# Windowed attention with a gated FFN on one core: own list scheduler for every engine, attention by half sequences

## The chip, the cores and the metric

The kernel runs on one core of one Trainium2 chip. The metric is the device time of one execution in microseconds (us), the median of several. A profiled execution has a span, from its first to its last instruction, about 2 us shorter than the time of that same execution. Engines: PE (TensorE), ACT (ScalarE), DVE (VectorE), POOL (GpSimd), SP (issues most DMAs); SPq is SP's DMA-issuing queue.

Each run is marked fast or slow, slow when it is more than 1.5% above the fastest run of the same kernel in its rounds; a single run's state is unknown. The rounds ran on different chips (1, 2 and 15), so versions of different rounds are compared by their ratios to the kernel before, which ran in every one of them.

## The reference, cut to what matters

Eight sequences of 576 tokens, 8 heads of 64. Attention sees 32 tokens to each side. Its output, as 512 columns, goes through a gated FFN: `h = relu(x w_in)` with 1024 columns, a depthwise convolution over three tokens, a sigmoid of that as a gate, and `w_out`.

```python
scores = q @ k.T / sqrt(64);  mask: |i - j| <= 32;  x = softmax(scores) @ v     # per head
h = maximum(x @ w_in, 0)
conv[t] = sum_k conv_w[k] * h[t + k - 1]
out = (h * sigmoid(conv)) @ w_out
```

Inputs and output are float32. The kernels compute in bfloat16. q, k and v are 9.4 MB each.

## The kernel before

Each batch's q and k are loaded four heads at a time, v in five blocks of 128 rows. POOL casts them to bfloat16. PE transposes q and k against an identity, computes scores for 64-query tiles against 128 keys ("sc", two at a time in the two halves of the array's rows), ACT takes the exponential, DVE multiplies by the mask, PE multiplies by V ("av", 64 output rows each), DVE divides by the sum. The FFN runs in 12 chunks of 384 tokens: ph (w_in), pc (convolution as matmuls with diagonal weights), py (w_out). A job list with start times, in part kept in program order, sets the order; the framework's scheduler does the rest.

The q/k load, whose rows matter most here. The source's outermost count is 128 and so is the tile's:

```python
def load_qk(b, y, i):
    src = (q, k)[y][b, 4 * i:4 * i + 4, :, :]
    fixed(nc.sync.dma_start(
        qkst[y][i].rearrange("p e j d -> p e (j d)"),              # 128 partitions
        bass.AP(src.tensor, src.offset, [[RP * D, 128], [2 * S * D, 2], [1, RP * D]]),
    ))                                                             # RP = 9: rows of 2304 bytes
```

PSUM is one buffer of three banks for scores and transposes, and five single banks.

The softmax here doesn't subtract the row's maximum and nothing guards it: scores larger than these inputs give would overflow.

Of the kernel before, what the change touches and what calls it, by code (L numbers as in the profile page):

```python
# [10 lines left out]
FP32 = mybir.dt.float32  # L11
BF16 = mybir.dt.bfloat16
AF = mybir.ActivationFunctionType
ALU = mybir.AluOpType


@with_exitstack
def kernel(
# [24 lines left out]
    RP = S // 64  # L43
# [3 lines left out]
    apool = ctx.enter_context(tc.tile_pool(name="apool", bufs=3))  # L47
    fpool = ctx.enter_context(tc.tile_pool(name="fpool", bufs=2))
    spool = ctx.enter_context(tc.tile_pool(name="spool", bufs=3))
    psum_a = ctx.enter_context(tc.tile_pool(name="psum_a", bufs=1, space=bass.MemoryType.PSUM))  # L50
    psum_f = ctx.enter_context(tc.tile_pool(name="psum_f", bufs=5, space=bass.MemoryType.PSUM))

    NLD = 2
    NPH = NP // 2
    qkst = [[pp.tile([128, 2, RP, 64], FP32, name=f"{n}st{i}") for i in range(NPH)] for n in "qk"]
    vst = pp.tile([128, NBLK, H, 64], FP32, name="vst")
    qkb_pp = [
        [[pp.tile([128, RP, 2, 64], BF16, name=f"{n}b{i}{j}") for j in range(NPH)] for n in "qk"]
        for i in range(NLD)
    ]  # L60
    ve_pp = [pp.tile([128, NBLK, H, 65], BF16, name=f"ve{i}") for i in range(NLD)]
    vo_pp = [pp.tile([128, NBLK - 1, H, 65], BF16, name=f"vo{i}") for i in range(NLD)]
    NKT = 4
    kT_pp = [pp.tile([128, S + 2 * PAD], BF16, name=f"kT{i}") for i in range(NKT)]
    hT_pp = [pp.tile([128, MB, CH + (4 if i == 1 else 2)], BF16, name=f"hT{i}") for i in range(3)]

    w_in_sb = consts.tile([128, KC, d_ff], BF16, name="w_in_sb")
    w_out_sb = consts.tile([128, MB, d_model], BF16, name="w_out_sb")
    conv_w_sb = consts.tile([128, 3, MB], FP32, name="conv_w_sb")
    diag_w = consts.tile([128, 3, MB, 128], BF16, name="diag_w")  # L70
    ident = consts.tile([128, 128], BF16, name="ident")
    mask = consts.tile([128, 2 * S], BF16, name="mask")
    mask1 = consts.tile([128, NT, 64], BF16, name="mask1")

    fixed = tc.keep_in_program_order

    class InOrder:


        on = False  # L80

        def __init__(self, engine):
            self.engine = engine

        def __getattr__(self, name):
            do = getattr(self.engine, name)
            return (lambda *args, **kwargs: fixed(do(*args, **kwargs))) if InOrder.on else do  # L87

    vector, scalar, tensor = InOrder(nc.vector), InOrder(nc.scalar), InOrder(nc.tensor)

    def load_v(b, c):

        lo = 128 * c - PAD
        s0, s1 = max(0, lo), min(S, lo + 128)
        fixed(nc.sync.dma_start(  # L95
            vst[s0 - lo:s1 - lo, c, :, :], v[b, :, s0:s1, :].rearrange("h p d -> p h d")
        ))

    def load_qk(b, y, i):


        src = (q, k)[y][b, 4 * i:4 * i + 4, :, :]
        fixed(nc.sync.dma_start(
            qkst[y][i].rearrange("p e j d -> p e (j d)"),
            bass.AP(src.tensor, src.offset, [[RP * D, 128], [2 * S * D, 2], [1, RP * D]]),
        ))

    def cast(out_, in_):
        fixed(nc.gpsimd.tensor_scalar(  # L109
            out=out_, in0=in_, scalar1=1.0, scalar2=0.0, op0=ALU.mult, op1=ALU.add  # L110
        ))

    def load_stream(b):

        i = b % NLD
        ve, vo = ve_pp[i], vo_pp[i]

        def cast_v(c):
            cast(ve[:, c, :, 0:64], vst[:, c, :, :])
            if b == 0 and c > 0:  # L120
                vector.tensor_copy(vo[0:64, c - 1, :, :], ve[64:128, c - 1, :, :])
                vector.tensor_copy(vo[64:128, c - 1, :, :], ve[0:64, c, :, :])

        of_qk = [
            (lambda y=y, j=j: load_qk(b, y, j),
             lambda y=y, j=j: cast(qkb_pp[i][y][j].rearrange("p j e d -> p e j d"), qkst[y][j]))
            for j in range(NPH) for y in range(2)
        ]
        of_v = [(lambda c=c: load_v(b, c), lambda c=c: cast_v(c)) for c in range(NBLK)]
        return of_qk + of_v  # L130

    def shift_v(b):

        ve, vo = ve_pp[b % NLD], vo_pp[b % NLD]
        for p0, src in ((0, ve[64:128, 0:NBLK - 1]), (64, ve[0:64, 1:NBLK])):
            fixed(nc.sync.dma_start(vo[p0:p0 + 64], src))
# [4 lines left out]
    loads0 = list(load_stream(0))  # L141
    for ld, _ in loads0:
        ld()
    conv_w24 = consts.tile([3 * MB, 128], FP32, name="conv_w24")
    nc.scalar.dma_start(conv_w24, moe_conv_w.rearrange("k (m p) -> (k m) p", p=128))
    make_identity(nc, ident)
    ident24 = consts.tile([3 * MB, 3 * MB], FP32, name="ident24")
    nc.vector.tensor_copy(out=ident24, in_=ident[0:3 * MB, 0:3 * MB])
    nc.vector.memset(mask1, 1.0)
    nc.gpsimd.affine_select(  # L150
        out=mask1, in_=mask1, compare_op=ALU.is_ge, fill=0.0, base=0,
# [3 lines left out]
        out=mask1, in_=mask1, compare_op=ALU.is_ge, fill=0.0, base=64,  # L155
        pattern=[[0, NT], [1, 64]], channel_multiplier=-1,
    )
    nc.vector.memset(mask1[0:PAD, 0, :], 0.0)
    nc.vector.memset(mask1[128 - PAD:128, NT - 1, :], 0.0)
    for e in range(2):  # L160
        nc.vector.tensor_copy(
            out=mask[:, 512 * e:512 * e + 512], in_=mask1[:, 0:8, :].rearrange("p t x -> p (t x)")
        )
        nc.vector.tensor_copy(out=mask[:, 1024 + 64 * e:1088 + 64 * e], in_=mask1[:, 8, :])
    for t_ in ve_pp + vo_pp[0:1]:
        nc.vector.memset(t_[:, :, :, 64], 1.0)
    for t_ in kT_pp:
        nc.vector.memset(t_[:, 0:PAD], 0.0)
        nc.vector.memset(t_[:, PAD + S:], 0.0)
    nc.vector.memset(hT_pp[0][:, :, 0], 0.0)  # L170
    nc.vector.memset(hT_pp[1][:, :, HW + 1:HW + 3], 0.0)
    nc.vector.memset(hT_pp[2][:, :, CH + 1], 0.0)
    def make_diag(m):
        for kk in range(3):
            vector.tensor_scalar(
                out=diag_w[:, kk, m, :], in0=ident,
                scalar1=conv_w_sb[:, kk, m:m + 1], scalar2=None, op0=ALU.mult,
            )

    def load_weight(src, dst, rows, cast_):  # L180

        n = src.shape[1] // 2
        for x in (0, n):
            st = {}

            def load(x=x, st=st):
                t_ = fpool.tile([128, rows * n], FP32, name="wst", tag="wst")
                st[0] = t_.rearrange("p (c f) -> p c f", c=rows)
                fixed(nc.sync.dma_start(
                    st[0], src.rearrange("(c p) f -> p c f", p=128)[:, :, x:x + n]  # L190
                ))

            def casts(x=x, st=st):
                step = 512 // n
                for c in range(0, rows, step):
                    cast_(dst[:, c:c + step, x:x + n], st[0][:, c:c + step])

            yield load, casts


    def slot_a():
        return psum_a.tile([128, 1536], FP32, name="pa", tag="pa")

    def slot_f():
        return psum_f.tile([128, 512], FP32, name="pf", tag="pf")

    xT, xn = {}, {}
    state = {}

    def job_tr(g2, y):  # L210

        b, i = g2 // NPH, g2 % NPH
        nat = qkb_pp[b % NLD][y][i]
        to = []
        for g in (2 * g2, 2 * g2 + 1):
            if y == 0:
                t_ = apool.tile([128, S], BF16, name="qT", tag="qT", bufs=4)
                to.append(t_)
            else:
                t_ = kT_pp[g % NKT]  # L220
                to.append(t_[:, PAD:PAD + S])
            state["qk"[y], g] = t_

        small = b == 0
        for js in ((range(0, 4), range(4, 8), range(8, RP)) if small else (range(RP),)):
            j0, n = js[0], len(js)
            ps = slot_f() if small else slot_a()
            for j in js:
                tensor.matmul(  # L229
                    ps[:, 128 * (j - j0):128 * (j - j0) + 128],  # L230
                    nat[:, j, :, :].rearrange("p e d -> p (e d)"),
                    ident, start=True, stop=True,
                )
            rows = ps[:, 0:128 * n].rearrange("p (j y x) -> p y x j", j=n, y=2)
            for x, copy in enumerate((scalar.copy, vector.tensor_copy)):
                copy(  # L236
                    out=to[x].rearrange("p (x j) -> p x j", j=RP)[:, :, j0:j0 + n], in_=rows[:, x]
                )

    def job_conv_w():  # L240
        ps = slot_f()
        tensor.matmul(ps[:, 0:3 * MB], conv_w24, ident24, start=True, stop=True)
        vector.tensor_copy(out=conv_w_sb.rearrange("p k m -> p (k m)"), in_=ps[:, 0:3 * MB])

    def head(pr, e):
        return 4 * (pr // 2) + pr % 2 + 2 * e
# [336 lines left out]
```

## Time and profile before

| | before |
|---|---|
| time, median of 3 runs | 275.63 us (274.66 to 276.86) |
| span of the profiled run | 271.7 us |
| PE busy | 236.4 us, 87% |
| DMA traffic | 49.6 MB |

From the page of the kernel before: PE's busy time, then busy tenths in 40 slices of 6.8 us (9 is 90% or more); PEclk is the clock granted to PE in tenths, DMA the busy share of 16 engines.

```profile
PE 236.4 (87%) x2535; PEld 143.5 (53%) x2562; DVE 160.5 (59%) x362; ACT 175.3 (65%) x370; POOL 81.0 (30%) x96
...
PE   1736974786999978998999999999999999999994
...
PEclk9999998998999997999999999999999999999998
DMA  7999999997377986399959988967546114312123
```

PE is at 9 from about a quarter of the span on. In front of that it is busy a little over half of the time, and there DMA is at 7 to 9: the start waits for bytes. The chain of waits of the first 50 us (start us, length us, what) says the same:

```profile
...
8.21 6.40 DMA vst<-in_v_dram
14.70 14.20 DMA kst<-in_k_dram
29.28 4.91 DMA vst<-in_v_dram
34.92 9.19 DMA vo<-ve
...
```

And this is the DMA view of 2 to 12 us, 40 slices of 0.25 us each. The q/k loads are in flight in its first half, then v:

```profile
DMA  8669999999999999999999999999999999999999
GB/s 94 203 251 412 378 341 406 406 424 406 406 387 378 406 378 406 387 378 406 415 396 415 415 387 362 328 287 221 188 211 193 164 154 206 218 216 220 216 218 216
```

During q/k loads the share reaches 9 tenths of 16 engines, at about 400 GB/s. The 256-byte rows of v come at about 215.

For the whole span the chain is PE's:

```profile
...
PE 68%; DMA 15%; DVE 5%; SPq 4%; ACT 3%; issue 2%; POOL 0%
...
```

### The profile page before, as it was taken

How to read it: one execution, taken by the hardware profiler on the slowest of the kernel's cores; microseconds unless marked ns; L12 is line 12 of the kernel's file. 1: busy time of each engine (PE TensorE's matmuls, PEld its weight loads, DVE VectorE, ACT ScalarE, POOL GpSimd, SP SyncE). 2: the span in 40 equal slices, each digit the busy share in tenths (PEclk: the TensorE clock that was granted, in tenths of full speed). 3: DMA queues.
4: the chain of work that ended last, by engine and by line, in shares of the span. 5: the costliest groups of instructions: out<-in, count | busy, mean ns of one | idle time of the engine just before them, and what ended most of it. 6: DMA issues, size and time to landing. Idle time of an engine off the chain costs nothing.

```text
span 271.7 us, 6447 instructions
## 1 busy us (share of the span) xinstructions
PE 236.4 (87%) x2535; PEld 143.5 (53%) x2562; DVE 160.5 (59%) x362; ACT 175.3 (65%) x370; POOL 81.0 (30%) x96
## 2 busy tenths in 40 slices
PE   1736974786999978998999999999999999999994
PEld 1625543574665544554555556565656455555551
DVE  5797385895466673765766656676666562323230
ACT  2755572585577663876777777777778567657552
POOL 5758656873026201233323432322300000000000
PEclk9999998998999997999999999999999999999998
DMA  7999999997377986399959988967546114312123
GB/s 258 256 344 358 198 296 321 224 309 164 100 183 253 222 151 165 110 287 242 208 146 319 159 196 257 294 112 177 152 121 89 40 41 109 98 39 77 41 77 116
DMA packets 70498, 49.64 MB, mean 183 GB/s; under 512 B 53676, under 2 KB 55748, under 8 KB 70468
## 3 DMA queue, kind: packets, MB, share of 16 engines
q1 hardware_dynamic: 70432, 49.22, 70.6%
q8 instruction: 20, 0.33, 0.6%
q14 instruction: 10, 0.08, 0.1%
q10 hardware_dynamic: 36, 0.01, 0.0%
HBM read 32.52 MB, written 9.44 MB: 154 GB/s over the span
## 4 chain that ended last, share of the span: by engine, by line
PE 68%; DMA 15%; DVE 5%; SPq 4%; ACT 3%; issue 2%; POOL 0%
PE pf L405 22%; PE pf L349 20%; PE pf L387 14%; DMA kst<-in_k_dram 5%; PE pa L229 4%; DMA vst<-in_v_dram 4%; PE pf L282 4%; DMA vo<-ve 3%; PE pa L257 3%; DMA xT<-xn 3%; SPq L95 2%; DVE attn L268 1%; SPq L312 1%; DVE gT L392 1%; DVE diag_w L87 1%
## 5 line engine op out<-in xcount | busy, mean ns | idle before, releaser
L392 DVE SCALAR_TENSOR_TENSOR gT<-tn,hT 128x384 bf16<-128x384 f32 (+1 forms) x96 | 55.7, 585 | 55.7 <-ACT tn L391 55.6
L349 PE MATMUL pf<-xT,w_in_sb 128*128 128x385 bf16 (+2 forms) x380 | 73.6, 317 | 4.9 <-DMA xT<-xn 3.7
L405 PE MATMUL pf<-w_out_sb,gT 128*128 128x512 bf16 x261 | 66.5, 385 | 1.7 <-issue 0.4
L387 PE MATMUL pf<-hT,diag_w 128*128 128x384 bf16 (+1 forms) x288 | 59.0, 314 | 0.7 <-ACT hT L360 0.6
L349 PEld LDWEIGHTS <-w_in_sb 128*128 128x128 bf16 x380 | 34.4, 98 | 25.9 <-issue 3.3
L410 ACT COPY y_sb<-pf 128x512 f32<-128x512 f32 x36 | 21.1, 586 | 40.8 <-PE pf L405 40.8
L391 ACT ACTIVATE tn<-pf 128x384 f32<-128x384 f32 (+1 forms) x96 | 44.9, 469 | 2.3 <-PE pf L387 1.9
L109 POOL TENSOR_SCALAR ve<-vst 128x512 bf16<-128x512 f32 x40 | 28.9, 724 | 55.2 <-DMA vst<-in_v_dram 42.9
L405 PEld LDWEIGHTS <-gT 128*128 128x128 bf16 x288 | 28.0, 99 | 30.4 <-issue 1.6
L387 PEld LDWEIGHTS <-diag_w 128*128 128x128 bf16 x288 | 26.1, 98 | 17.1 <-issue 1.2
L369 ACT ACTIVATE hT<-pf 128x385 bf16<-128x385 f32 x56 | 27.7, 496 | 10.8 <-PE pf L349 10.1
L266 ACT ACTIVATE attn<-pa 128x1088 bf16<-128x1088 f32 x26 | 27.9, 1074 | 4.7 <-PE pf L257 3.9
L109 POOL TENSOR_SCALAR qb<-qst 128x1152 bf16<-128x1152 f32 x16 | 19.9, 1242 | 26.8 <-DMA qst<-in_q_dram 26.8
L268 DVE TENSOR_TENSOR attn<-attn,mask 128x1152 bf16<-128x1152 bf16 x26 | 20.9, 804 | 10.4 <-ACT attn L267 9.6
L109 POOL TENSOR_SCALAR kb<-kst 128x1152 bf16<-128x1152 f32 x16 | 18.9, 1182 | 21.9 <-DMA kst<-in_k_dram 21.1
L301 DVE TENSOR_TENSOR xn<-pf,rec 128x320 bf16<-128x320 f32 x52 | 24.3, 486 | 0.8
L364 ACT ACTIVATE hT<-pf 128x386 bf16<-128x386 f32 x24 | 11.9, 494 | 4.4 <-PE pf L349 4.0
L282 PEld LDWEIGHTS <-attn 128*64 128x64 bf16 x520 | 10.7, 112 | 7.3 <-issue 5.6
L282 PE MATMUL pf<-ve,attn 128*64 128x65 bf16 x312 | 13.8, 199 | 0.3 <-DVE attn L268 0.3
L257 PEld LDWEIGHTS <-kT 64*128 64x128 bf16 x468 | 9.0, 95 | 7.9 <-issue 5.5
L257 PE MATMUL pa<-qT,kT 64*128 64x64 bf16 x442 | 12.3, 191 | 0.9 <-DVE kT L236 0.9
L282 PE MATMUL pf<-vo,attn 128*64 128x65 bf16 x208 | 12.9, 200 | 0.0
(84 smaller groups left out, 240.1 us busy)
## 6 DMA issues: line engine op xcount, KB each, us to landing
qst<-in_q_dram SPq DMA_DIRECT2D x16, 576.0 KB, 6.4
kst<-in_k_dram SPq DMA_DIRECT2D x16, 576.0 KB, 7.4
out_dram<-y_sb SPq DMA_DIRECT2D x36, 256.0 KB, 2.2
vst<-in_v_dram SPq DMA_DIRECT2D x24, 256.0 KB, 4.7
vo<-ve SPq DMA_DIRECT2D x14, 260.0 KB, 7.8
vst<-in_v_dram SPq DMA_DIRECT2D x16, 192.0 KB, 5.0
wst<-in_moe_w_in_dram SPq DMA_DIRECT2D x2, 1024.0 KB, 8.4
wst<-in_moe_w_out_dram SPq DMA_DIRECT2D x2, 1024.0 KB, 8.9
```

What stands on the lines that cost most here:

```text
L109: fixed(nc.gpsimd.tensor_scalar(out=out_, in0=in_, scalar1=1.0, scalar2=0.0, op0=ALU.mult, op1=ALU.add))
L257: tensor.matmul(last[:, 0:64] if e * t == NT - 1 else ps[:, col(e, t):col(e, t) + 64], kT[64 * e:64 * e + 64, 64 * t:64 * t + 128], qT[64 ...
L266: scalar.activation(attn[:, 0:x], ps[:, 0:x], AF.Exp, bias=0.0, scale=scale)
L268: vector.tensor_tensor(out=attn, in0=attn, in1=mask, op=ALU.mult)
L282: tensor.matmul(pss[e][64 * j:64 * j + 64, 65 * c:65 * c + 65], attn[:, col(e, t):col(e, t) + 64], (ve if t % 2 == 0 else vo)[:, t // 2, h ...
L301: vector.tensor_tensor(out=to, in0=po[:, :, 0:64], in1=rec[:, :, None].broadcast_to([128, NBLK, 64]), op=ALU.mult,)
L349: tensor.matmul(ps[:, 0:n], w_in_sb[:, kc, m * 128:(m + 1) * 128], x_[:, kc, x0:x1], start=(kc == 0), stop=(kc == KC - 1),)
L369: scalar.activation(hT[:, m, o0:o0 + n], ps[:, 0:n], AF.Relu, bias=0.0, scale=0.5)
L387: tensor.matmul(ps[:, 0:n], diag_w[:, kk, m, :], taps(kk), start=(kk == 0), stop=(kk == 2))
L391: scalar.activation(tn[:, 0:n], ps[:, 0:n], AF.Tanh, bias=0.0, scale=1.0)
L392: vector.scalar_tensor_tensor(out=gT[c][:, m, HW * halves[0]:HW * halves[0] + n].rearrange("p (i x) -> p i x", x=HW), in0=tn[:, 0:n].rearr ...
L405: tensor.matmul(ps, gT[c][:, m, 128 * i:128 * i + 128], w_out_sb[:, m, :], start=(m == 0), stop=(m == MB - 1),)
```

## The change

Its intent: PE should start earlier and never wait. All instructions become operations of a plan; a list scheduler in the kernel places each at the earliest time by costs fitted to traces, chooses among allowed engines and PSUM banks (any of 8), and emits them in exactly that order. Attention goes by half sequences of 288 tokens, so that the FFN can begin after half a sequence; head g stands beside head g + 4. A few jobs change engine: the diagonal weights go to POOL, the V shift of sequence 1 goes from DMA to DVE. The diff, cut to its core:

```diff
-    qkst = [[pp.tile([128, 2, RP, 64], FP32, ...) for i in range(NPH)] for n in "qk"]
+    st = [[pp.tile([128, 2, RP, D], FP32, name=f"{n}st{s}") for s in range(2)] for n in "qk"]
+    ps_all = psum.tile([128, 8 * 512], FP32, name="ps_all")
...
+    def load_qk(b, y, s, prio):                # half s of all heads; NP = 4, HS = 288, RP = 9
+        src = (q, k)[y][b]
+        for h_ in range(2):
+            add(sp(), prio + 0.01 * h_, lambda e, h_=h_: nc.sync.dma_start(
+                st[y][s][:, h_].rearrange("p j d -> p (j d)"),
+                bass.AP(
+                    src.tensor, src.offset + HS * D * s + NP * S * D * h_,
+                    [[S * D, NP], [RP * D, 32], [1, RP * D]],
+                ),
+            ), writes=[("st", y, s, h_)], dma=0.77)
...
+    def transposes(b, s):                      # copies out of PSUM
+        copy(e, o_, ps(sl, 128 * a, 128 * (a + n)).rearrange("p (j g x) -> p g x j", j=n, x=32))
...
+    def values(b, s, g, t):                    # one PE group for each half and head pair
+        add(("PE", 0.02 * 4 * n), t, mm, ..., alloc=sl, slots=[sl], group=gr)
...
+    with tc.manual_schedule():
+        for op in plan.place():
+            op.run(op.eng)
```

## The prediction

> **What bounds the kernel now.** Span 271.7 us; runs take about 4 us more (median 275.6). The windows show two stages. From 64 to 264 us PE is 97% busy. In the first 64 us it is busy 39 us, with modelled ends, so I recount by start-to-start distances in the timeline: 216 ns for a 512-column matmul, 163 for 384, 56 for 128, about 18 for an attention matmul (they overlap in pairs). [...] In the first 30 us the trace shows 107 ns for 128 columns[...]. All matmuls at these distances come to about 211 us (estimate), so about 61 us are lost: 38 by 64 us, 10 to 16 from there to 260, 8 at the end.
>
> Why 38: the chain of waits is nearly all DMA up to 44 us (V load 6.4, K load 14.2, V load 4.9, the vo shift of sequence 1 9.2 us). DMA is nearly saturated there (about 0.27 MB per us), so what counts is the order of bytes. The first FFN matmul starts only at about 24 us because all of sequence 0 comes first; PE stands still from 40 to 44; until 68 it waits on evictions, one 3-bank buffer shared by transposes and scores, and 9 us of diag_w on DVE.
>
> **What the change does.** Matmul work, bytes and evicted elements stay nearly equal. It moves:
> - Half sequences: estimate from 0.27 MB/us: half 0 in at 9 us, w_in at 16, half 1 at 22, w_out at 29, sequence 1 at 35 and 42. First FFN matmul at about 16 us.
> - The b=1 vo shift goes from DMA (9.2 us) to DVE copies (0.3 us each); diag_w to POOL.
> - PSUM: any of 8 banks, no single 3-bank buffer. ACT loses 32 exponentials of 64 columns (0.22 us each), off the critical path.
> - Order on every engine fixed by a model whose costs match the trace (DVE 384 elements 476 ns, ACT 512 elements 489).
>
> **Sum.** With loads in at about 42 us, PE cannot have done more than chunks 0 and 1 and two sequences (38 us of work) by about 52; I expect 18 to 20 us lost by then, against 34 now: about 15 saved. Steady state (17.6 us of PE work per chunk; ACT about 67%, DVE 60%) should lose 6 to 10 after 52 instead of about 18: 8 to 10 saved. Tail (three output tiles, 5.2 us of matmuls, copy, store) unchanged. Total about 24: span 247, time 251 us, range 242 to 263.
>
> Chances: faster by over 2% 0.91, within 2% 0.06, slower 0.03.
>
> **What would show it.** First w_in matmul at 14 to 18 us; no PE hole near 40; PE slices at 9 from about 48 us; last chunk's start about 20 us earlier; chain without vo DMA before 50 us and almost all PE after; PE busy still about 236. POOL gains about 7 us (diag_w), DVE loses about 9.
>
> **What would make it wrong.** A fixed order that the chip's DMA does not follow: loads later than the plan's 0.77 us per 295 KB[...]. [...] diag_w on POOL could take longer than its 2.4 us and delay the casts. SP issues in order, so a store or transpose that waits can hold up loads. Those push to 263 or above.

Of the prediction are cut: a formula for the distance between matmuls, a cause given for the 107 ns (the clock granted in those 30 us is 1.00 of full speed), and two risks that rested on the same cause or on a mechanism that is not shown. That a store that waits can hold up loads is in the trace of before: from 58.8 to 69.9 us SPq issues nothing; then comes the store of what ACT has just copied, and 0.06 us after that issue a V load.

## The result, and the profile after

The kernel after takes 380.94 us (median of 4 runs, 380.15 to 381.59) against 275.14 us in the same rounds. The ratio is 1.383, 95% interval 1.377 to 1.389. Here and below a ratio is the mean of one kernel's fast runs over that of the other's fast runs in the same rounds, so not quite the ratio of the medians. The result is correct. It is 38% slower where 9% faster was forecast.

```profile
PE 264.3 (70%) x2618; PEld 156.8 (41%) x2618; DVE 168.5 (44%) x394; ACT 174.9 (46%) x348; POOL 71.9 (19%) x86
...
PE   0246526748492790592199937978769899999996
...
PEclk9999865867967796597589975989969999999999
DMA  2564375444455434736984369595369621321112
```

Now PE has holes over three quarters of the span, and DMA is mostly at 3 to 6, not at 9. Both are waiting. The DMA's half share is no sign of slack, as the view of 2 to 12 us shows beside that of before:

```profile
DMA  0221132122222222222235998322222222222368
GB/s 0 37 37 46 37 74 65 65 101 101 92 92 101 101 92 92 101 92 111 92 122 177 256 259 190 93 92 92 111 92 111 92 101 101 101 101 92 119 182 225
```

Wherever only q/k packets run, the share is 2 tenths and the rate 92 to 101 GB/s. Counted packet by packet in the trace, 4.2 are in flight at a time in these stretches, against about 16 in the kernel before. A packet is the same in both (2304 bytes, a median of 95 ns, before 93). So in these stretches a quarter as many packets move at a time. The chain of waits of the whole execution:

```profile
...
DMA 34%; SPq 32%; PE 23%; issue 3%; POOL 3%; DVE 2%; ACT 2%; POOLq 0%; ACTq 0%
SPq L369 14%; DMA qst<-in_q_dram 10%; SPq L344 9%; PE ps_all L739 8%; DMA kst<-in_k_dram 7%; DMA vst<-in_v_dram 7%; DMA out_dram<-y 7%; PE ps_all L668 7%; PE ps_all L698 6%; SPq L397 4%; DMA xT<-xn 2%; SPq L571 2%; SPq L412 2%; POOL qn L252 1%; POOL ve L252 1%
...
```

and some of its pieces between 50 and 130 us:

```profile
...
53.71 12.80 DMA qst<-in_q_dram
...
72.71 9.01 DMA qst<-in_q_dram
...
83.05 3.83 SPq L344
...
87.95 9.17 DMA qst<-in_q_dram
...
```

A q load of 288 KB accounts for 9 to 13 us of the chain at a time. SPq itself stands in issuing: single q/k issues took up to 5.9 us, in the kernel before at most 1.2. What held such an issue the trace does not say, and one of 5.0 us comes in the repaired version below too. With PE starved, its granted clock is lower as well (0.856 on average against 0.978). PE's busy time went up, 236.4 to 264.3 us, though by the recount's distances its matmuls need the same 211 us in both (an estimate); the repaired version below has the same 2618 matmuls, a clock of 0.975 and 240.2 us.

### The profile page after: what moved, and what is told of

It reads as the page before. It is cut to its first block, busy times and chain, and to the rows that moved or that the text cites. A ratio compares the mean times of both kernels' runs of the same rounds, so it can differ in the third digit from the quotient of the medians.

```text
span 379.9 us, 6745 instructions
## 1 busy us (share of the span) xinstructions
PE 264.3 (70%) x2618; PEld 156.8 (41%) x2618; DVE 168.5 (44%) x394; ACT 174.9 (46%) x348; POOL 71.9 (19%) x86
## 4 chain that ended last, share of the span: by engine, by line
DMA 34%; SPq 32%; PE 23%; issue 3%; POOL 3%; DVE 2%; ACT 2%; POOLq 0%; ACTq 0%
SPq L369 14%; DMA qst<-in_q_dram 10%; SPq L344 9%; PE ps_all L739 8%; DMA kst<-in_k_dram 7%; DMA vst<-in_v_dram 7%; DMA out_dram<-y 7%; PE ps_all L668 7%; PE ps_all L698 6%; SPq L397 4%; DMA xT<-xn 2%; SPq L571 2%; SPq L412 2%; POOL qn L252 1%; POOL ve L252 1%
## 5 line engine op out<-in xcount | busy, mean ns | idle before, releaser
L668 PE MATMUL ps_all<-xT,w_in_sb 128*128 128x385 bf16 (+4 forms) x448 | 88.8, 337 | 22.5 <-DMA xT<-xn 20.9
L715 DVE SCALAR_TENSOR_TENSOR gT<-tn,hT 128x384 bf16<-128x384 f32 (+3 forms) x112 | 58.0, 527 | 78.5 <-ACT tn L708 78.2
L684 ACT ACTIVATE hT<-ps_all 128x385 bf16<-128x385 f32 (+4 forms) x112 | 50.3, 459 | 51.1 <-PE ps_all L668 50.0
L739 PE MATMUL ps_all<-w_out_sb,gT 128*128 128x512 bf16 x288 | 72.7, 399 | 0.0
L698 PE MATMUL ps_all<-hT,diag_w 128*128 128x384 bf16 (+3 forms) x336 | 69.4, 326 | 3.4 <-ACT hT L684 3.2
L708 ACT ACTIVATE tn<-ps_all 128x384 f32<-128x384 f32 (+3 forms) x112 | 49.9, 452 | 20.8 <-PE ps_all L698 17.0
L750 ACT COPY y<-ps_all 128x512 f32<-128x512 f32 x36 | 21.1, 586 | 79.9 <-PE ps_all L739 45.5
L256 DVE CAST qT<-ps_all 128x512 bf16<-128x512 f32 (+1 forms) x41 | 29.1, 725 | 30.4 <-PE ps_all L442 30.4
L506 ACT ACTIVATE attn<-ps_all 128x1024 bf16<-128x1024 f32 (+1 forms) x40 | 36.7, 946 | 5.2 <-PE ps_all L493 5.1
L521 DVE TENSOR_TENSOR attn<-attn,mask 128x1024 bf16<-128x1024 bf16 (+1 forms) x48 | 26.3, 567 | 20.9 <-ACT attn L506 20.1
L560 DVE TENSOR_TENSOR xn<-ps_all,rec 128x256 bf16<-128x256 f32 (+1 forms) x64 | 30.3, 484 | 1.0
```

The source lines that it names most:

```text
L506: add(act(2 * w), t + 0.1, lambda e: nc.scalar.activation(at, ps(sl, 0, 1024).rearrange("p (e x) -> p e x", e=2)[:, :, 0:w], AF.Exp, bias= ...
L668: nc.tensor.matmul(ps(sl, 0, n), w_in_sb[:, kc, m * 128:(m + 1) * 128], x_[:, kc, a0:a1], start=(kc == 0), stop=(kc == KC - 1),)
L684: nc.scalar.activation(o_, i_, AF.Relu, bias=0.0, scale=0.5)
L698: nc.tensor.matmul(ps(sl, 0, no), diag_w[:, kk, m, :], hview(m, o0, o1, kk - 1), start=(kk == 0), stop=(kk == 2),)
L708: add(act(no), tt + 0.1, lambda e, sl=sl, r=r: nc.scalar.activation(tn[r][:, 0:no], ps(sl, 0, no), AF.Tanh, bias=0.0, scale=1.0), reads=[s ...
L715: nc.vector.scalar_tensor_tensor(out=gT[ig][:, m, o0:o1].rearrange("p (i x) -> p i x", i=i2), in0=tn[r][:, 0:no].rearrange("p (i x) -> p i ...
```

## The experiments

Three theories. A: each q/k load runs on 4 of the 16 DMA engines, because of its access pattern: 4.2 packets are in flight, and 4 is the outermost count of the source, where it was 128 with about 16 in flight. That the one sets the other was the estimate until the runs below. B: the fixed order of the own list scheduler makes engines wait. C: the single issue queue, with stores behind loads.

### Sixteen engines for the q/k loads

The source lists its 32 rows outermost and its four heads inside; the transposed columns then come as (x g) instead of (g x), and the copies read them so. The plan does not change.

```diff
-                    [[S * D, NP], [RP * D, 32], [1, RP * D]],
+                    [[RP * D, 32], [S * D, NP], [1, RP * D]],
...
-                        "p (j g x) -> p g x j", j=n, x=32))
+                        "p (j x g) -> p g x j", j=n, x=32))
```

> The kernel after, with one thing changed: the q and k loads list their rows with 32 as the outermost count instead of 4 (and the copies out of PSUM read the transposed columns in that order). Same bytes, same plan, same number of instructions. Theory A (each q/k load runs on only 4 of the 16 DMA engines, because the outermost count of its source is 4): q/k packets run about 16 at a time instead of 4.2, 0.39 MB per us instead of 0.10, and the time falls below the kernel before, to 244 to 262 us as forecast. Theory B [...]: time stays above 340 us whatever the loads do. Theory C (the single in-order issue queue, with stores behind blocked loads): partial recovery, 280 to 340 us.

Measured: 275.35 us, before in the same rounds 276.01; ratio 1.003 (0.994 to 1.012). Two counts exchanged in one line, with the copies to match, take away 106 of 381 us.

```profile
DMA  0976999989998558999999999999979999998999
GB/s 0 166 157 221 378 387 369 406 332 203 249 240 203 157 194 303 300 327 306 263 198 202 235 196 186 202 168 161 123 121 249 283 300 289 271 229 262 377 401 401
```

The share is back at 9 tenths, at about 400 GB/s in the q/k stretches; v comes between them because half sequences take turns. B and C are out as causes of the 38%. But the time is 275 us and not the 244 to 262 that theory A went on to promise. That is a second question, taken up below.

### The fault alone, in the kernel before

Each q/k load is cut at row 124, so that the outermost counts are 124 and 4 instead of 128. That 124 would do as 4 does was the estimate; this run tests it.

```diff
-        fixed(nc.sync.dma_start(qkst[y][i]..., [[RP * D, 128], ...]))
+        for p0, p1 in ((0, 124), (124, 128)):
+            fixed(nc.sync.dma_start(qkst[y][i][p0:p1]..., [[RP * D, p1 - p0], ...]))   # offset + RP * D * p0
```

> The kernel before, with each q/k load cut into rows 0 to 123 and rows 124 to 127. [...] Nothing else changes. Theory A: 4 engines carry all q/k bytes; from the trace of before, 925 us of q/k packet time over 4 engines is 231 us, plus 2177 us of other packets over 16 engines, 136 us: these four engines alone need up to 367 us, so the kernel before becomes slow like the kernel after, 340 to 410 us. Theories B and C (the order of the new kernel is at fault): 272 to 285 us, as nothing of the new order is in it.

Measured: 399.18 us, ratio 1.453 (1.438 to 1.468). Nothing of the new order is in this kernel, and it has the same disease, mostly 2 tenths and in the last 3 us of the view 83 to 111 GB/s:

```profile
DMA  1411211223222223131322223231222222222222
GB/s 47 37 37 37 55 65 76 95 94 101 74 55 74 65 65 74 46 92 46 92 55 83 65 74 83 65 92 65 101 83 92 92 101 92 111 83 92 101 92 101
```

### Two engines

```diff
-                st[y][s][:, h_]...,      [[S * D, NP], [RP * D, 32], [1, RP * D]]
+                st[y][s][64 * g:64 * g + 64, h_]..., [[S * D, 2], [RP * D, 32], [1, RP * D]]   # for g in range(2)
```

> The kernel after with each q/k load cut into two loads of two heads each, so that the outermost count of the source is 2. Theory A: 2 engines per load, about 2.1 packets at a time and 0.05 MB per us during q/k loads; the q/k packets take 858 us of engine time, 429 on two engines instead of 215 on four, so about 215 us longer than the kernel after: 540 to 640 us. If the slowness were a matter of the order or of the number of bytes in flight: about 380.

Measured in one run (its state is unknown, as of any single run): 562.87 us, with 2.1 packets in flight:

```profile
DMA  0011112000101111111111111111111111111111
GB/s 4 28 37 55 37 55 37 28 18 37 46 37 46 55 55 46 46 55 55 55 46 46 55 55 55 46 46 55 55 46 55 46 55 55 46 46 55 55 46 46
```

The rates during q/k loads are about 0.40 MB per us with an outermost count of 128 (before) or 32 (sixteen engines), 0.10 with 4, 0.08 with 124 and 4 (mean of 2 to 12 us), and 0.05 with 2: in proportion to the packets in flight where they were counted (about 16 with 128, 4.2 with 4, 2.1 with 2). What other counts do is not shown. The estimate from engine time held roughly. q/k packets take 858 us of engine time in the trace of after, 215 us on four engines; on two it is 215 us more, and the time rose by 182. The trace does not number the engines; it shows only that the number in flight is about 2 or 4 and that the rate goes with it.

### Sixteen engines by smaller loads

The layout in SBUF stays as in the kernel after; each load becomes four of one head (32 rows, 74 KB).

```diff
-   one dma_start of 128 partitions, source [[S * D, NP], [RP * D, 32], [1, RP * D]]
+   four dma_starts of 32 partitions, source [[RP * D, 32], [1, RP * D]]
```

> The kernel after with the same layout of rows in SBUF and the same plan, but each q/k load issued as 4 loads of one head, 32 rows each [...]. Four times as many q/k issues (256 instead of 64). Theory A: 16 engines per load, time 246 to 275 us, perhaps a few us over the sixteen-engine version for the issues (about 0.45 us each on the queue, 192 more of them, 86 us more of queue time that is mostly idle otherwise). If instead the layout of partitions (which head's rows sit where) were the cause: no recovery, above 340.

Measured: 313.96 us, ratio 1.144 (1.133 to 1.155). Most of the loss is gone, so the count and not the layout is the cause, but the 246 to 275 expected is missed. The DMA view shows why:

```profile
DMA  6548183637455474726653647465524799999999
GB/s 226 166 129 240 65 230 111 212 102 194 129 184 129 157 166 157 230 65 175 166 184 120 194 129 194 120 194 120 166 58 111 170 279 282 267 243 224 216 217 196
```

The first 7 us of q/k loads come at about 0.157 MB per us: SPq needs 0.46 us for each issue (16 issues in 7.3 us), and 74 KB per 0.46 us is 0.16 MB per us. The queue, not the engines, is the limit there. I had counted its issues as hidden. Over the whole execution SPq is 16% of the chain of waits, in the sixteen-engine version 1%; that all 39 us between the two versions are the queue's is not shown.

### Where the forecast gain went

With the loads repaired the kernel ties with before. To see where PE's time goes I recount as the prediction did: each matmul at its streaming distance, from its start to that of the next in an unbroken stream (211 us in all), and what is left of a stretch as lost. The trace of before lacks 27 matmul records of py, 5.8 us, all after 52 us; the first column corrects for them.

| lost us | before | sixteen engines | prediction for after |
|---|---|---|---|
| 0 to 52 us | 33.8 | 35.1 | 18 to 20 |
| 52 to 260 us | 22.6 | 23.2 | less than before by about 10 |

Neither of the two savings is there.

```profile
PE 240.2 (88%) x2618; PEld 145.8 (53%) x2618; DVE 180.7 (66%) x394; ACT 174.5 (64%) x348; POOL 76.8 (28%) x86
...
PE   0449644998899998899999999999999999999994
...
PEclk9999875899999999999999999999999999999999
DMA  6999899899998999999994888332121321302012
```

```profile
...
PE 71%; DVE 20%; ACT 3%; DMA 2%; issue 1%; SPq 1%; ACTq 0%; DVEq 0%
...
```

**The start.** First the kernel before, then the sixteen-engine version, by stretch: the columns are busy us of each engine.

```profile
core 0: us, PE busy (x) PEld busy (x) DVE busy (x) ACT busy (x) POOL busy (x), PEclk, DMA share, GB/s
24.00:48.00 24.00, 17.32 (x172) 10.99 (x172) 14.57 (x36) 13.66 (x34) 15.83 (x21) 0.94 1.00 281
48.00:64.00 16.00, 12.10 (x212) 9.50 (x210) 14.64 (x33) 10.85 (x28) 11.20 (x12) 0.99 1.04 261
```

```profile
core 0: us, PE busy (x) PEld busy (x) DVE busy (x) ACT busy (x) POOL busy (x), PEclk, DMA share, GB/s
24.00:48.00 24.00, 14.48 (x215) 11.72 (x213) 21.45 (x40) 13.96 (x27) 15.26 (x18) 0.75 0.97 272
48.00:64.00 16.00, 16.00 (x213) 12.04 (x212) 9.77 (x30) 9.95 (x31) 2.98 (x4) 0.95 0.92 259
```

The first w_in matmul does come earlier, at 20.7 instead of 28.6 us. But then, from 24 to 48 us, DVE is busy 21.4 of 24 us, and PE does less than before, at a lower clock (PEclk 0.75). It catches up from 48 to 64 us, but from 64 to 84 us DVE is busy 19.2 of 20 us and the lead is gone again: 42.5 us lost by 84 us, before 42.3 (with its two missing records of that stretch). DVE is not only given more to do, its instructions take longer than the plan counts. Here are V shift copies, all of one size (start us, length us). At 12.27 us POOL stood idle; at 30.15, 34.09 and 38.48 it was casting:

```profile
...
12.27 0.29 DVE L392 COPY vo<-ve 64x520 bf16<-64x520 bf16 x1
...
30.15 0.59 DVE L392 COPY vo<-ve 64x520 bf16<-64x520 bf16 x1
...
34.09 0.59 DVE L392 COPY vo<-ve 64x520 bf16<-64x520 bf16 x1
...
38.48 0.59 DVE L392 COPY vo<-ve 64x520 bf16<-64x520 bf16 x1
...
```

Sorted by whether POOL worked during at least 60% of the instruction or during none (medians in ns, sixteen-engine version):

```
DVE instruction                          POOL idle    POOL busy
V shift, copy 64x520, SBUF                  291          602
mask, 128x1024, two SBUF inputs             693         1089
gate, 128x192, two SBUF inputs              347          793
divide, 128x384, from PSUM                  557          545
copy 128x512, from PSUM                     725          716
```

Of these five, the copy within SBUF and the two with two SBUF inputs take longer beside a busy POOL, the two that read PSUM do not. Why is not shown. The trace also shows the wait itself, in POOL's casts and the DVE copies that started during them:

```profile
...
39.52 1.15 POOL L252 TENSOR_SCALAR qn<-qst 128x1152 bf16<-128x1152 f32 x1
...
39.75 1.06 DVE L392 COPY vo<-ve 64x520 bf16<-64x520 bf16 x1
...
41.44 0.62 POOL L252 TENSOR_SCALAR ve<-vst 128x512 bf16<-128x512 f32 x1 [0.77 <-DMA vst<-in_v_dram]
41.54 0.67 DVE L392 COPY vo<-ve 64x520 bf16<-64x520 bf16 x1
...
```

All six shift copies that start during a cast end 0.14 to 0.15 us after that cast ends, whether they took 0.59 or 1.06 us; six of the seven such masks of 1024 columns end 0.53 to 0.54 us after it. So these instructions do not run at a slower rate, they wait for the end of the cast, and the medians of the table depend on how long the casts happen to be. The plan had 0.35 us for the shift and 0.61 for the mask, whatever POOL does. So its order had DVE free sooner than the chip did.

The first edit against this gives the plan the long times for the first two sequences and lets ScalarE help:

```diff
-   add(dve(H * (D + 1), 2), ...shift...)
+   add(dict([dve(H * (D + 1)), act(H * (D + 1))]), ...shift...)                  # sequences 0, 1
-   add(dve(2 * w, 2), t + 0.2, masks, ...)
+   add(dve(2 * w, 2 if b > 1 else 1), t + 0.2, masks, ...)
-   on = ... if name == "w_in" else pool(512)
+   on = ... if name == "w_in" else dict([act(512), pool(512)])                   # casts of w_out
```

> The sixteen-engine version with three changes for the first two sequences: the shift of V may run on ScalarE too, the plan is told the longer VectorE times that the trace shows beside a busy GpSimd (shift 0.60 us instead of 0.29, mask 1.09 instead of 0.69), and the casts of w_out may run on ScalarE too. Theory E (the first 50 us are held by VectorE, which is slowed while GpSimd works, and by its fixed order): 2 to 8 us less, 267 to 273 us, with less VectorE in the chain of waits before 50 us. Rival (the first 50 us are held by the arrival of the bytes): no change, within 1 us.

Measured: 269.59 us, ratio 0.976 (0.967 to 0.984) to before; three of the six runs are marked slow and are in the median, not in the ratio. The two halves of this edit were then run apart. The plan's numbers only:

```diff
-   add(dve(H * (D + 1), 2), ...shift...)
+   add(dve(H * (D + 1)), ...shift...)
-   add(dve(2 * w, 2), t + 0.2, masks, ...)
+   add(dve(2 * w, 2 if b > 1 else 1), t + 0.2, masks, ...)
```

> One half of the start-up edit alone: the sixteen-engine version with only the plan's numbers changed for the first two sequences (V shift 0.62 us instead of 0.35, mask 1.14 instead of 0.61, as VectorE takes beside a busy GpSimd). No instruction moves to another engine by edit; only order and the plan's own choices can change. If a wrong cost in the plan was what held the start: 269 to 272 us. If the load on VectorE itself was: 274 to 277, as in the sixteen-engine version (275.4).

Measured: 269.59 us, ratio 0.986 (0.980 to 0.992). And the engines only, with the plan's numbers as they were (the shift is now given to ScalarE, where the joint edit let the plan choose):

```diff
-   add(dve(H * (D + 1), 2), ...shift...)
+   add(act(H * (D + 1)), ...shift...)
-   on = ... if name == "w_in" else pool(512)
+   on = ... if name == "w_in" else dict([act(512), pool(512)])
```

> The other half alone: the 16 copies of the V shift of the first two sequences on ScalarE instead of VectorE, and the w_out casts on ScalarE or GpSimd; costs in the plan as they were. If load on VectorE held the start: 268 to 272 us. If the plan's costs did: 274 to 277.

Measured: 272.94 us, ratio 1.000 (0.994 to 1.005); the time lies between the two forecasts. From the sixteen-engine version's 1.003 the true numbers bring 1.7%, ScalarE 0.3%, which its interval doesn't separate from nothing. That ScalarE adds anything to the true numbers isn't shown either: both medians are 269.59 us, and the intervals of the two ratios overlap. Not one instruction was edited to another engine for the true numbers, only the order and the plan's own choices changed (with them the plan took five of 394 instructions off DVE). The same stretches with the true numbers:

```profile
core 0: us, PE busy (x) PEld busy (x) DVE busy (x) ACT busy (x) POOL busy (x), PEclk, DMA share, GB/s
24.00:48.00 24.00, 19.24 (x313) 15.25 (x311) 21.48 (x46) 19.22 (x48) 17.40 (x21) 0.93 1.14 297
48.00:64.00 16.00, 13.77 (x204) 10.42 (x203) 12.75 (x29) 12.38 (x28) 7.21 (x8) 1.00 1.03 263
```

PE does 19.2 us there instead of 14.5, with DVE as busy as it was. Lost by 52 us: 28.9 us instead of 35.1. Of these 6.2 us, 2.4 are matmuls at half rate (107 ns apart for 128 columns where 56 is usual): by the recount they cost 5.3 us by 52 us in the sixteen-engine version and 2.9 here. What keeps the other ten of the forecast 15 us from coming stays open.

**Steady state.** Of the 23.2 us lost from 52 to 260 us, about 15 lie at steps between a 64-wide attention matmul and a full-array one, or between the two attention shapes. Lines of the sixteen-engine version (start us, length us) around one attention group:

```profile
...
151.73 0.82 PE L668 MATMUL ps_all<-xT,w_in_sb 128*128 128x385 bf16 x4
...
152.47 0.20 PEld L540 LDWEIGHTS <-attn 128*64 128x64 bf16 x8 [0.32 <-issue]
...
152.60 0.20 PE L540 MATMUL ps_all<-vo,attn 128*64 128x65 bf16 x1
...
152.72 1.90 PE L739 MATMUL ps_all<-w_out_sb,gT 128*128 128x512 bf16 x8
...
```

The last w_in matmul of the four starts about 0.26 us before the attention group and streams for 0.16; the weight load stands 0.32 us in front of the group; and the last attention matmul is followed by the w_out one 0.12 us later, where attention matmuls inside the group need about 0.017 each. Over the whole span such a step costs about 105 ns over the streaming distance. A step between two kinds of full-array matmul, from w_in to convolution say, costs nothing (a median of 0.2 ns over 157 steps after 64 us). The kernel before has 119 steps between tile shapes, the sixteen-engine version 159: attention by halves makes 13 groups a sequence where it was 8. So a change of tile shape costs time here where a change between full-array kinds does not; why is not shown.

```diff
-            for g in range(NP):
-                values(b, s, g, when(b, s, 0.58 + 0.1 * g))
+            for gs in ([(0, 1), (2, 3)] if b > 1 else [(g,) for g in range(NP)]):
+                values(b, s, gs, when(b, s, 0.58 + 0.1 * gs[-1]))     # a slot of len(gs) banks
```

> The sixteen-engine version with the attention-times-V matmuls of two head pairs issued as one group from the third sequence on (two adjacent banks instead of one). Same matmuls. In the traces a step between a 64-wide attention matmul and a full-array matmul, or between the two attention shapes, costs about 105 ns over the streaming distance (before: 119 such steps, 11.7 us where short; sixteen-engine version: 159 steps, 15.4 us). Theory D (the switches ate part of the forecast gain): 24 groups fewer, 48 steps, 5.0 us: about 270 us. Rival (PE has slack elsewhere, or two adjacent banks are harder to get): 274 us or more.

Measured: 273.98 us, ratio 0.996 (0.990 to 1.001). The steps fell from 159 to 128 in the recorded matmuls (26 records are missing), the sum of the short ones by 3.8 us of the 5.0 expected, but the time fell by about 0.7%, 2 us, and the interval overlaps that of the sixteen-engine version. The step's cost is seen in the trace; that taking steps away returns all of it is not shown. In the two profiled runs the time lost from 52 to 260 us did fall by 3.4 us, from 23.2 to 19.8 (with the missing records counted), but the fast runs of this version spread over 272.2 to 274.5 us. So it stays open whether a part is lost elsewhere; two adjacent banks may be harder to get.

Together with the start edit, both diffs as above:

> Both of the above together. They act in different stages (after about 60 us, and before 50 us), so if both theories hold the gains add: 262 to 269 us, at least 2% under the kernel before. If only one holds: 268 to 273.

Measured: 266.00 us (median of 7 runs), ratio 0.968 (0.963 to 0.974): the best version, faster than both kernels. Beside the start edit alone (0.976, same rounds) pairs bring 0.7% here too, again with overlapping intervals.

Then two steps further in the same direction:

```diff
-   add(dve(2 * w, 2 if b > 1 else 1), t + 0.2, masks, ...)
+   add(dve(2 * w, 1), t + 0.2, masks, ...)
-   if b > 1:
+   if b > 3:
        on = dict([act(128 * n) if n_ % 2 else dve(128 * n)])        # copies of q and k out of PSUM
```

> Both edits together (266.0 us) with two more in the same direction: the plan counts all masks at the slow rate, not only those of the first two sequences, and for the third and fourth sequence the copies out of PSUM may go to either engine instead of alternating. VectorE was busy 86% of 50 to 110 us there, beside a GpSimd that casts, and PE lost 13 us in 60 to 100 us. If that is VectorE's load: 261 to 265 us. If PE's 64-wide work and its switches fill that stretch: 265 to 268.

Measured: 265.63 us, ratio 0.971 (0.967 to 0.975), level with the last one. The 261 to 265 expected from VectorE's load did not come; the time lies in the range of the rival, 265 to 268. The page of this version:

```profile
...
PE 235.0 (89%) x2618; PEld 143.9 (54%) x2618; DVE 171.0 (64%) x374; ACT 184.9 (70%) x367; POOL 77.3 (29%) x87
...
PE   0449759997988997999999999999999999999994
...
```

Lost by 52 us are 29.0 us in this version, between 52 and 260 us 21.1, of which the steps are 10 to 12 (by where one counts a long gap as something else).

### The fixed order itself

```diff
-    with tc.manual_schedule():
-        for op in plan.place():
-            op.run(op.eng)
+    for op in plan.place():
+        op.run(op.eng)
```

> The sixteen-engine version, with the operations handed to the framework's scheduler in the plan's order instead of being fixed in it. Buffers, PSUM banks and data flow as in the plan; only the order on the engines is the framework's. If the own order brings part of the gain: 255 to 290 us, slower than the fixed order by 5 us or more. If the gain comes from half sequences and banks alone: within 2% of the fixed order.

Measured: 288.60 us, ratio 1.051 (1.043 to 1.060), against 1.003 with the order fixed. So, as expected, the fixed order is no fault: with this data flow it saves 13 us.

## Why the prediction was wrong, point by point

- **The step that failed** is "Matmul work, bytes and evicted elements stay nearly equal", followed by "estimate from 0.27 MB/us: half 0 in at 9 us". The bytes were equal (49.1 and 49.6 MB), the rate was not: 127 GB/s over the first 20 us, 0.10 MB per us in q/k loads. I took a rate from one access pattern and gave it to another: an estimate from the trace of before, applied where the trace of before has no such load. The diff shows the outermost count of 4 where the kernel before has 128; I did not ask whether the rate would hold for it. This is 106 of the 130 us between forecast and result. The other 24 are the gain that was not there:
- The text did also name "loads later than the plan's 0.77 us per 295 KB" as a risk. One such load has 128 packets of 95 ns; on four engines that is 3.0 us (an estimate from the trace of after). The risk was right in kind, wrong in its weight: the chance of slower was 0.03.
- "First w_in matmul at 14 to 18 us": 28.4 in the kernel after, 20.7 once repaired. The 24 us that I gave for the kernel before were wrong too: its trace has 28.6 (its plan says 23).
- "I expect 18 to 20 us lost by then, against 34 now: about 15 saved": with the loads repaired, none (33.8 and 35.1 lost). The shift at "0.3 us each" takes 0.60 beside a busy POOL, and "a model whose costs match the trace" matches instructions that run while POOL is idle: it has no term for a cast beside them, though three of the eight shift copies in the trace of before took 0.59 to 0.61 us. With true numbers 5 of the 15 us come (33.8 to 28.9). In terms of the prediction: the overlap of VectorE with GpSimd was taken as free, and the trace shows VectorE's shift copies and masks waiting until the cast ends (0.15 and 0.54 us past it).
- Steady state "should lose 6 to 10 after 52 instead of about 18": 23 us to 260 alone, in both. I left out the steps between tile shapes, 12 us over the span of the kernel before and 15 in the repaired version; the change adds groups. What else the steady state loses, about 8 of the repaired version's 23.2 us, is not shown.
- "PE busy still about 236": 264.3, at a lower clock; 240.2 once repaired. "POOL gains about 7 us, DVE loses about 9": POOL lost 9 (81.0 to 71.9), DVE gained 8 (160.5 to 168.5), and 20 in the repaired version. The plan put eleven casts of the start on DVE (three on ACT), and its shift copies and masks wait for POOL's casts (602 and 1089 ns beside a busy POOL, 291 and 693 beside an idle one).
- "no PE hole near 40": there is one even once repaired, PE is busy 14.5 of 24 us there.

## What to carry to other kernels

Cost a DMA by its access pattern, not by its bytes: read the outermost counts (here 128 and 32 gave about 0.40 MB per us in loads of 288 KB and more, 4 gave 0.10 and 2 gave 0.05), and look in the first microseconds of the DMA view whether the share is full (9 tenths here) or a fraction (2 tenths with 4, 1 with 2). A DMA share of a half (51% in the kernel after) with every engine waiting came here from loads with 4.2 packets in flight, not from slack. A fixed order is as good as its numbers: take them from the conditions under which the instruction will run, with POOL busy beside it where it will be. Here a copy of 0.29 us took up to 1.06, as long as the cast beside it had left plus 0.15.
